# A fused linear-attention and feed-forward kernel: w_out words loaded 18 steps ahead, one q buffer per unit, and the left half of a group's output buffer in two pieces

## The chip, the core and the metric

The kernel runs on one core of a Trainium2 chip. The metric is device time in microseconds, the median of the runs of one kernel. The profile is one execution of the same program, recorded instruction by instruction; its times count from its own first instruction. TensorE is called PE, VectorE DVE, ScalarE ACT, GpSimd POOL and SyncE SP. SP does no arithmetic here: it issues nearly all transfers, one after the other. ACT issues the others, the stores of the middle result.

## The reference

The computation is linear attention with a norm for each head, followed by a feed-forward block without bias.

```python
kv = np.einsum('bhsd,bhse->bhde', k, v)           # batch 8, 8 heads, 576 tokens, head_dim 64
out = np.einsum('bhsd,bhde->bhse', q, kv)
rms = np.sqrt(np.mean(out * out, axis=-1, keepdims=True) + 1e-06)
x = (out / rms * g_norm)                          # reordered to 4608 tokens x 512
h = x @ w_in                                      # w_in 512 x 2048
sp = np.log1p(np.exp(h))                          # h itself above 20
out = (h * np.tanh(sp)) @ w_out                   # w_out 2048 x 512
```

The arrays are handed over as 64-bit floating point. The kernel reads the two weight matrices as pairs of 32-bit words and rebuilds a 32-bit value from each pair.

## The kernel before

**Two parts.** Part one goes through nine tiles of 512 tokens. For each tile it computes the attention, the first product and the activation, and stores the activated result in device memory (`gd`). Part two reads `gd` back in 18 pieces of 256 tokens and computes the second product. Part two starts about two thirds into the program, and no line of its loop is part of the change, but for the name of one buffer (`o_dst`, L607).

**Steps.** The first product of a tile is cut into four groups, and a group is computed with seven block products instead of eight (Strassen's scheme with sums and differences of blocks). One block product is one *step*: 12 matmuls at L411. So a group has 7 steps and a tile 28 (`NS`). The functions `p0` to `p6` (L371 to L398) are the steps of a group. They also move the accumulator out of PSUM: ACT copies blocks (L374, L379, L388), DVE adds blocks (L429), and ACT applies the activation, called Mish here (L116).

**The plan.** All other work is hung on a step number with `at(step, f)`, and `trace(step)` emits it when the step has been emitted: attention of the *next* tile (`attention(j)`, L498), conversion of `w_out` (L527), loads and stores. SP's order is exactly this order of emission. The orders on PE, ACT and DVE are made by a scheduler that estimates when each instruction can start; an engine then runs its list strictly in that order. A wait on one engine holds up all that stands behind it in the list.

**Attention.** A tile's attention is done in two units of four heads (two head pairs of two). A unit loads q (`load`, L267, eight pieces of one or two transfers), transposes it on DVE (L287), projects it with the product of k and v on PE (L299 to L304), squares (ACT, L308), sums over a head with a matrix of ones (PE, L319 to L322), takes the logarithm and the exponential on ACT (L327, L328) and multiplies on DVE (L332). From the third tile on, operands are split into a high and a low part first (`split`, L118: ACT L119, DVE L120). The logarithm and exponential need one table set on ACT and Mish another; each change is an `ACT_TABLE_LOAD`. Both units load q into one buffer, `qs`, so the second unit's load can't be issued before the first unit's transpose has read it.

**k and v.** They are loaded in four portions per tile (L206, L207), with one staging buffer for each. A portion is loaded when the product of the portion before it (L242) has been emitted.

**w_out.** Its conversion is cut into 16 halves (`weight_forms`, L126). Half `i` is loaded into a raw buffer (`w64`, two of them; L136), scaled on ACT (L141), joined on DVE (L146 to L148), turned into differences (L153 to L155), split into `wst` (one buffer; L119, L120) and stored in device memory (`wod`, L193). Half `i` is due 12 steps after half `i-1`. The line that sets the steps is

```python
for s, n in enumerate((-8, 0, 1, 2, 3, 4, 6)):   # load, scale, join, differences, first, rest, store
    at(max(NS, NS + 12 * i + n), run)
```

`w_in` is converted in the same way during the first tile, without a store, and before any attention needs the split buffers.

**The output buffers of a group.** `ul` (left 256 columns' two blocks: 11 and 21) and `ur` (12 and 22) hold 128 x 1024 values each, two of each. Block 11 is finished in step 5 of its group, block 22 in step 6, and block 21 in step 2 of the next group. `ur` is stored from step 7 on, counted from the group's start, and all of `ul` from step 10 on (L434, L427). The first write into the `ul` of a group two later is at step 14 (L374).

Of the kernel before, what the change touches and what calls it, by code (L numbers as in the profile page):

```python
# [29 lines left out]
def linear_attention_rms_mish_ffn(  # L30
# [95 lines left out]
    def weight_forms(srcs, m, n, forms, put=None):  # L126
# [10 lines left out]
            st["w"] = t.rearrange("p b n t -> p (b n) t")  # L137

        def scale():
            st["x"] = wpools["wx"].tile([P, 4 * w], F32, name="wx")  # L140
            nc.scalar.mul(st["x"], st["w"][:, :, 1].bitcast(F32), 2.0 ** -112)  # L141

        def join():
# [120 lines left out]
    def unit_steps(j, u):  # L264
        st = {}

        def load(n):  # L267
            if n == 0:
                st["q"] = att.tile([P, 2, T], F32, name="qs")
            a, i = divmod(n, 4)  # L270
            h, d0 = 4 * u + 2 * a + i // 2, 32 * (i % 2)
            for b, s0, cols in segments(j):
                n_ = cols.stop - cols.start
                nc.sync.dma_start(
                    st["q"][32 * i:32 * i + 32, a, cols].rearrange("p (c d) -> p c d", d=32),
                    q[b, h, s0:s0 + n_, d0:d0 + 32].rearrange("(c p) d -> p c d", p=32),
                )
# [137 lines left out]

    def u_dst(st, block):

        for name in ("ul", "ur"):
            if name not in st:
                st[name] = up.tile([P, 2, T], F32, name=name)  # L420
        return st["ul" if block[1] == "1" else "ur"][:, :, (int(block[0]) - 1) * TH:int(block[0]) * TH]

    def put_in(st, block, bank):
        o, i, n, t = u_dst(st, block), st["i"], st["n"], 7 * (NQ * st["i"] + st["n"])
        if block == "21":
            mish(o, bank)
            at(t + 10, lambda: nc.scalar.dma_start(gd[i][:, 2 * n:2 * n + 2, :], st["ul"]))  # L427
            return
        nc.vector.tensor_add(o, bank, o)  # L429
        if block == "11":  # L430
            mish(o, o)
        elif block == "22":
            mish(st["ur"], st["ur"])
            at(t + 7, lambda: nc.scalar.dma_start(gd[i][:, NF2 + 2 * n:NF2 + 2 * n + 2, :], st["ur"]))  # L434


    NS = 7 * NQ
# [12 lines left out]
    weight_pools(2, 1, 0)  # L450
    kv_new(0)
    rooms = [up.tile([P, 4, CM * D], F32, name=n) for n in ("ul", "ul", "ur", "ur")]
    units = {j: [unit_steps(j, u) for u in range(2)] for j in range(NT)}
    conv, kv_tiles = {}, {}
    for step in START.split():
# [8 lines left out]
        elif what == "k":  # L464
            ts = []
            for m in range(2):
                ts.append(rooms[2 * n + m])
                ts.append(x[0:SL, 2 * n + m, 0:4 * D].rearrange("p (h d) -> p h d", h=4))
# [29 lines left out]
    def attention(j):  # L498
# [14 lines left out]
        for u, ns in enumerate(((3, 5, 6, 8, 9, 10), (12, 14, 15, 17, 18, 19))):  # L513
            for s, n in enumerate(ns):
                at(t + n, units[j][u][s + 1])
            for n in range(8):
                at(t + 4 + n if u else max(t - 15 + 2 * n, n // 2 - 1), lambda u=u, n=n: units[j][u][0](n))
        at(t + 20, lambda: x_sums(0))
        for f, n in zip(range(7), (21, 22, 24, 25, 26, 27, 30)):
            at(t + n, lambda f=f: x_form(f))  # L520
# [4 lines left out]
        attention(j)  # L525
    at(NS - 1, lambda: weight_pools(2, 1, 1))
    for i in range(2 * NF2):  # L527
        for s, n in enumerate((-8, 0, 1, 2, 3, 4, 6)):
            def run(i=i, s=s):
                if s == 0:  # L530
                    conv["out", i] = weight_out(i // 2, i % 2)
                conv["out", i][s]()
            at(max(NS, NS + 12 * i + n), run)
# [70 lines left out]

    def o_dst(st, block):
        if "o" not in st:
            st["o"] = up.tile([P, 2, DM], F32, name="ul")  # L607
        r, c = int(block[0]) - 1, int(block[1]) - 1
        return st["o"][:, r, c * G:(c + 1) * G]

# [140 lines left out]
```

## Time and profile before

| | us |
|---|---|
| median of 3 runs (lowest, highest) | 957.74 (954.23, 961.63) |
| the profiled execution, its own time | 965.35 |
| the profiled execution, span of its instructions | 963.6 |
| PE busy / ACT busy / DVE busy in that span | 858.5 / 510.3 / 596.3 |
| part one up to the last steps of the first product | 0 to about 598 |
| part two in its steady course | 618.7 to the end |

How to read the rows of the views shown below. In a row of the list of instructions in time, the first number is the start, the second the length of the instructions merged in the row, then the engine (SPq and ACTq are the queues on which SP and ACT issue transfers), the line, the operation, what it writes and reads, and a count; in brackets stands how long the engine had been idle before, and what ended that. In the view of waits a row has the total of such idle times, their number and the longest. In the view of stretches a row has the stretch, its length, then the busy time of PE, of PE's weight loads, DVE, ACT and POOL, with the number of instructions, then the granted PE clock (1.00 is full speed), the busy share of the transfer engines, and GB/s.

### The profile page before, as it was taken

The numbers are of one execution on the slowest core, as the hardware profiler recorded it, in microseconds if no ns is written. First come the engines' busy times: TensorE is split into PE (matmuls) and PEld (weight loads), VectorE is DVE, ScalarE is ACT, GpSimd is POOL, SyncE is SP. The second block draws the span as 40 slices with busy tenths as digits, with TensorE's granted clock in tenths as the row PEclk, the third lists the DMA queues.
The fourth block names the chain that finished last, engine by engine and source line by source line (L and its number), as shares of the span: only waits on it lengthen the run. The fifth ranks groups of instructions, "written<-read, shape, count | busy, mean of one in ns | idle before, by whom it ended". The sixth has DMA issues, their size and how long they took to land.

```text
span 963.6 us, 16994 instructions
## 1 busy us (share of the span) xinstructions
PE 858.5 (89%) x6940; PEld 823.7 (85%) x6940; DVE 596.3 (62%) x832; ACT 510.3 (53%) x776; POOL 3.6 (0%) x14
## 2 busy tenths in 40 slices
PE   3587899698895987979989799799999999999998
PEld 1376798697895986978989699799999999999997
DVE  3777964637456556374764445766677766777762
ACT  2666775666556655665676535334444344444341
POOL 1000000000000000000000000000000000000000
PEclk9797999899996997989999899899999999999999
DMA  9567475666466665665653779634433345333421
GB/s 189 160 181 201 127 215 154 199 180 169 151 166 185 173 175 179 177 167 184 183 170 127 256 304 350 248 110 150 157 110 132 110 141 165 110 132 110 133 87 44
DMA packets 204461, 160.49 MB, mean 167 GB/s; under 512 B 91232, under 2 KB 189536, under 8 KB 203360
## 3 DMA queue, kind: packets, MB, share of 16 engines
q1 hardware_dynamic: 194016, 121.67, 43.4%
q10 hardware_dynamic: 10368, 37.75, 10.1%
q8 instruction: 54, 0.88, 0.4%
q14 instruction: 23, 0.19, 0.1%
HBM read 97.52 MB, written 61.87 MB: 165 GB/s over the span
## 4 chain that ended last, share of the span: by engine, by line
PE 44%; DMA 6%; ACT 2%; DVE 1%; issue 1%; SPq 0%; ACTq 0%
PE a L600 20%; PE bc L600 15%; PE a L411 4%; PE bc L411 3%; DMA g<-gd 2%; DMA gd<-ul 2%; DMA wf<-wod 1%; PE q L668 1%; DMA vm<-in_v_dram 1%; DMA wod<-wst 1%; DVE gf L120 0%; DMA w<-in_moe_w_out_dram 0%; ACT L116 0%; ACT fa L328 0%; ACT ur L116 0%
## 5 line engine op out<-in xcount | busy, mean ns | idle before, releaser
L411 PE MATMUL a<-gf,wf 128*128 128x256 f32 x1728 | 254.8, 302 | 49.2 <-ACT ul L116 18.0
L411 PEld LDWEIGHTS a<-gf,wf 128*128 128x128 f32 x1728 | 236.4, 207 | 60.1 <-ACT ul L116 20.2
L600 PE MATMUL a<-wf,gf 128*128 128x256 f32 x1632 | 204.7, 286 | 4.7 <-ACT ul L374 3.8
L600 PEld LDWEIGHTS a<-wf,gf 128*128 128x128 f32 x1632 | 200.8, 194 | 5.3 <-ACT ul L374 4.0
L411 PE MATMUL bc<-gf,wf 128*128 128x256 f32 x1296 | 183.3, 292 | 7.6 <-ACT ur L379 3.2
L411 PEld LDWEIGHTS bc<-gf,wf 128*128 128x128 f32 x1296 | 170.0, 198 | 11.4 <-ACT ur L379 4.7
L600 PE MATMUL bc<-wf,gf 128*128 128x256 f32 x1224 | 153.2, 284 | 1.2 <-DVE gf L120 1.2
L600 PEld LDWEIGHTS bc<-wf,gf 128*128 128x128 f32 x1224 | 149.9, 193 | 1.4 <-DVE gf L120 1.4
L120 DVE TENSOR_TENSOR gf<-g,gf 128x1024 fp32r<-128x1024 f32 (+1 forms) x100 | 109.6, 1103 | 64.9 <-ACT gf L119 64.7
L119 ACT CAST gf<-g 128x1024 fp32r<-128x1024 f32 (+1 forms) x100 | 94.4, 953 | 60.4 <-PE bc L600 55.2
L119 ACT CAST gf<-s 128x1024 fp32r<-128x1024 f32 (+2 forms) x58 | 49.1, 849 | 34.0 <-PE a L600 29.3
L120 DVE TENSOR_TENSOR gf<-s,gf 128x1024 fp32r<-128x1024 f32 (+2 forms) x58 | 56.3, 972 | 14.2 <-ACT gf L119 14.0
L374 ACT COPY ul<-a 128x512 f32<-128x512 f32 (+1 forms) x53 | 27.2, 516 | 60.2 <-PE a L600 29.3
L429 DVE TENSOR_TENSOR ur<-bc,ur 128x512 f32<-128x512 f32 x36 | 24.8, 688 | 37.6 <-PE bc L411 29.6
L116 ACT ACTIVATE ur<-ur 128x1024 f32<-128x1024 f32 x36 | 37.8, 1050 | 12.3 <-DVE ur L429 12.3
L146 DVE TENSOR_SCALAR wx<-wx 128x512 uint32<-128x512 uint32 (+1 forms) x24 | 12.3, 513 | 51.3 <-ACT wx L141 51.3
L120 DVE TENSOR_TENSOR fl<-fa,fh 128x1024 fp32r<-128x1024 f32 x28 | 34.2, 1220 | 13.5 <-ACT fh L119 13.4
L429 DVE TENSOR_TENSOR ur<-a,ur 128x512 f32<-128x512 f32 x36 | 24.7, 685 | 27.2 <-PE a L411 27.1
L141 ACT ACTIVATE wx<-w 128x512 f32<-128x512 f32 (+1 forms) x24 | 19.8, 826 | 38.3 <-DMA w<-in_moe_w_out_dram 29.9
L429 DVE TENSOR_TENSOR ul<-bc,ul 128x512 f32<-128x512 f32 x36 | 24.8, 688 | 24.7 <-ACT ul L374 16.1
L119 ACT CAST fh<-fa 128x1024 fp32r<-128x1024 f32 x28 | 29.3, 1047 | 16.8 <-DVE fa L287 16.6
L120 DVE TENSOR_TENSOR gf<-gf 128x512 fp32r<-128x512 f32 x45 | 29.9, 682 | 8.9 <-ACT gf L119 8.9
(95 smaller groups left out, 846.4 us busy)
## 6 DMA issues: line engine op xcount, KB each, us to landing
g<-gd SPq DMA_DIRECT2D x18, 2048.0 KB, 8.8
gd<-ur ACTq DMA_DIRECT2D x36, 512.0 KB, 4.1
gd<-ul ACTq DMA_DIRECT2D x36, 512.0 KB, 4.9
wod<-wst SPq DMA_DIRECT2D x16, 896.0 KB, 5.4
wf<-wod SPq DMA_DIRECT2D x8, 1792.0 KB, 12.0
out_dram<-ul SPq DMA_DIRECT2D x18, 512.0 KB, 2.8
w<-in_moe_w_in_dram SPq DMA_DIRECT2D x32, 256.0 KB, 3.9
w<-in_moe_w_out_dram SPq DMA_DIRECT2D x32, 256.0 KB, 3.5
```

Source lines behind the costliest of these rows:

```text
L116: in_turn(nc.scalar.activation(o, i, AF.Mish))
L119: nc.scalar.copy(hi, src)
L120: nc.vector.tensor_sub(lo, src, hi.bitcast(F32))
L141: nc.scalar.mul(st["x"], st["w"][:, :, 1].bitcast(F32), 2.0 ** -112)
L146: nc.vector.tensor_single_scalar(t, t, 3, ALU.logical_shift_left)
L374: nc.scalar.copy(dst(st, "11"), st["a"])
L411: nc.tensor.matmul(bank[:, jj], w[:, right, a, kc, :], xf[:, b, kc, :], start=first and jj == kc == s == 0, stop=(kc == 1 and s == 2), ski ...
L429: nc.vector.tensor_add(o, bank, o)
L600: nc.tensor.matmul(bank, gf[:, a, c, :], wo[c][:, right, b, :], start=first and c == s == 0, stop=(c == NF2 - 1 and s == 2), skip_group_ch ...
L668: nc.tensor.matmul(banks[b][:, h], gf[:, a, c, :], wo[2 * n + c][:, right, d, :], start=n == c == s == h == 0, stop=last_one, skip_group_c ...
```

## The change

Three things are changed, and some rooms move to make space.

1. **w_out words.** The load of half `i` moves from 8 to 18 steps before its conversion, and the store from 6 to 5 steps behind the conversion's start. The halves 0 and 1 are both loaded at the first step of the second tile.
2. **q buffers.** `qs` becomes `qs0` and `qs1`, one for each unit (a unit is a pair of head pairs). The first unit's pieces are loaded at 24 to 3 steps before the tile's steps, three steps apart (before: 15 to 1, two apart); the second unit's at 15 steps before to 6 steps into them, three apart (before: 4 to 11 steps into them, one apart).
3. **Left half.** `ul` is replaced by `ula` (block 11, first 256 tokens) and `ulb` (block 21, the other 256). Block 11 is stored on ACT's queue from step 6 on, block 21 from step 10 on, so a group has three stores and no longer two. A piece of the left half holds 256 KB and goes to rows of 1 KB in two places per partition; the whole left half was 512 KB.

The rooms: the scaled words of `w_in` use `fl`, a buffer of the attention, and `wx` is opened for `w_out` alone; the first tile's second portion of k and v is loaded into `x`, where the tile's result is later written; part two's output buffer is now called `ur`.

```diff
-            st["x"] = wpools["wx"].tile([P, 4 * w], F32, name="wx")
+            st["x"] = (wpools["wx"] if put else att).tile([P, 4 * w], F32, name="wx" if put else "fl")
...
-                st["q"] = att.tile([P, 2, T], F32, name="qs")
+                st["q"] = att.tile([P, 2, T], F32, name=f"qs{u}")
...
-        for name in ("ul", "ur"):
-            if name not in st:
-                st[name] = up.tile([P, 2, T], F32, name=name)
-        return st["ul" if block[1] == "1" else "ur"][:, :, (int(block[0]) - 1) * TH:int(block[0]) * TH]
+        name, shape = {"11": ("la", TH), "21": ("lb", TH)}.get(block, ("r", T))
+        if name not in st:
+            st[name] = up.tile([P, 2, shape], F32, name="u" + name)
+        return st[name] if name != "r" else st[name][:, :, (int(block[0]) - 1) * TH:int(block[0]) * TH]
...
         if block == "21":
             mish(o, bank)
-            at(t + 10, lambda: nc.scalar.dma_start(gd[i][:, 2 * n:2 * n + 2, :], st["ul"]))
+            at(t + 10, lambda: nc.scalar.dma_start(left[:, :, TH:T], o))
             return
         nc.vector.tensor_add(o, bank, o)
         if block == "11":
             mish(o, o)
+            at(t + 6, lambda: nc.scalar.dma_start(left[:, :, 0:TH], o))
...
-    rooms = [up.tile([P, 4, CM * D], F32, name=n) for n in ("ul", "ul", "ur", "ur")]
+    rooms = [up.tile([P, 4, CM * D], F32, name="ur") for _ in range(2)]
+    rooms += [x[:, 2 * u:2 * u + 2].rearrange("p a (h n) -> p (a h) n", h=2) for u in range(2)]
...
-                at(t + 4 + n if u else max(t - 15 + 2 * n, n // 2 - 1), lambda u=u, n=n: units[j][u][0](n))
+                at(max(t - (15 if u else 24) + 3 * n, n // 2 - 1), lambda u=u, n=n: units[j][u][0](n))
...
-        for s, n in enumerate((-8, 0, 1, 2, 3, 4, 6)):
+        for s, n in enumerate((-18, 0, 1, 2, 3, 4, 5)):
```

**What moves on SP.** The place is in the third tile, where the first portion of k and v of the fifth tile is issued. `km`, `kr`, `vm`, `vr` are the staging buffers of k and v, `qs` the q buffer, `w_...` a raw buffer of `w_out`, `wod_100` the stored forms. Before:

```order
L206 DMA km<-in_k_dram 128x2x256
L207 DMA kr<-in_k_dram 64x2x64
L206 DMA vm<-in_v_dram 128x2x256
L207 DMA vr<-in_v_dram 64x2x64
L274 DMA qs<-in_q_dram 32x6x32
L274 DMA qs<-in_q_dram 32x10x32
L136 DMA w_2060<-in_moe_w_out_dram 128x2x256 x2
L274 DMA qs<-in_q_dram 32x8x32 x2
L193 DMA wod_100<-wst 1792x1x128
L274 DMA qs<-in_q_dram 32x8x32 x10
L136 DMA w_2304<-in_moe_w_out_dram 128x2x256 x2
```

At the same place now:

```order
L206 DMA km<-in_k_dram 128x2x256
L207 DMA kr<-in_k_dram 64x2x64
L206 DMA vm<-in_v_dram 128x2x256
L207 DMA vr<-in_v_dram 64x2x64
L274 DMA qs_1864<-in_q_dram 32x8x32 x4
L274 DMA qs_2102<-in_q_dram 32x8x32 x2
L193 DMA wod_100<-wst 1792x1x128
L136 DMA w_2135<-in_moe_w_out_dram 128x2x256 x2
L274 DMA qs_1864<-in_q_dram 32x8x32 x2
L274 DMA qs_2102<-in_q_dram 32x8x32 x2
```

The store is that of half 3 in both. Before, the load of half 4 (`w_2060`) stood just ahead of it, and that of half 5 (`w_2304`) ten q transfers behind it. Now half 4 has been loaded further up, half 5 (`w_2135`) is loaded right behind the store, and the q transfers of the two units alternate.

**What moves on ACT.** The place is the end of the first tile and the start of the second. The numbers tell buffers apart: `ul_906`, `ul_1040` and `ul_1261` belong to three groups in a row, `a` is an accumulator, `gd0` and `gd1` the stored results of the first two tiles. Before:

```order
L119 CAST wst_1111<-w64_1062 128x4x128
L427 DMA gd0_90<-ul_906 128x1024
L250 CAST kvh0_1043<-s2_1125 64x64
L116 ACTIVATE ul_1040<-ul_1040 128x2x256
L116 ACTIVATE ur_1041<-ur_1041 128x1024
L374 COPY ul_1261<-a_1248 128x2x256
L434 DMA gd1_91<-ur_1041 128x1024
L308 ACTIVATE fa_1239<-x2_1195 128x1024
L141 ACTIVATE wx_1391<-w64_1177 128x512
```

Now, for the first of these three groups:

```order
L374 COPY ula_921<-a_908 128x512
L119 CAST wf_859<-w64_719 128x4x256
L119 CAST gf_108<-gf_107 128x512
L119 CAST gf_110<-gf_107 128x512
L116 ACTIVATE ula_921<-ula_921 128x512
L434 DMA gd0_90<-ula_921 128x2x256
L379 COPY ur_939<-bc_926 128x2x256
L119 CAST gf_108<-s1_904 128x512
```

Before, the copy into `ul_1261`, which takes the space of `ul_906`, stood four rows behind the store of `ul_906`. Now the store of `ula_921` follows its Mish at once, and the copy that takes its space, into `ula_1284`, stands 25 rows further down.

More of the change, by code (lines that the diff above doesn't have):

```diff
@@ L416, in u_dst @@
     def u_dst(st, block):
-        for name in ("ul", "ur"):
-            if name not in st:
-                st[name] = up.tile([P, 2, T], F32, name=name)
-        return st["ul" if block[1] == "1" else "ur"][:, :, (int(block[0]) - 1) * TH:int(block[0]) * TH]
+        name, shape = {"11": ("la", TH), "21": ("lb", TH)}.get(block, ("r", T))
+        if name not in st:
+            st[name] = up.tile([P, 2, shape], F32, name="u" + name)
+        return st[name] if name != "r" else st[name][:, :, (int(block[0]) - 1) * TH:int(block[0]) * TH]
     def put_in(st, block, bank):
         o, i, n, t = u_dst(st, block), st["i"], st["n"], 7 * (NQ * st["i"] + st["n"])
+        left, right = gd[i][:, 2 * n:2 * n + 2, :], gd[i][:, NF2 + 2 * n:NF2 + 2 * n + 2, :]
         if block == "21":
             mish(o, bank)
-            at(t + 10, lambda: nc.scalar.dma_start(gd[i][:, 2 * n:2 * n + 2, :], st["ul"]))
+            at(t + 10, lambda: nc.scalar.dma_start(left[:, :, TH:T], o))
             return
@@ L431, in put_in @@
             mish(o, o)
+            at(t + 6, lambda: nc.scalar.dma_start(left[:, :, 0:TH], o))
         elif block == "22":
-            mish(st["ur"], st["ur"])
-            at(t + 7, lambda: nc.scalar.dma_start(gd[i][:, NF2 + 2 * n:NF2 + 2 * n + 2, :], st["ur"]))
+            mish(st["r"], st["r"])
+            at(t + 7, lambda: nc.scalar.dma_start(right, st["r"]))
     NS = 7 * NQ
@@ L449, in linear_attention_rms_mish_ffn @@
     nc.gpsimd.memset(ones[D:P, D:P].bitcast(F32), 1.0)
-    weight_pools(2, 1, 0)
+    weight_pools(2, 0, 0)
     kv_new(0)
-    rooms = [up.tile([P, 4, CM * D], F32, name=n) for n in ("ul", "ul", "ur", "ur")]
+    rooms = [up.tile([P, 4, CM * D], F32, name="ur") for _ in range(2)]
+    rooms += [x[:, 2 * u:2 * u + 2].rearrange("p a (h n) -> p (a h) n", h=2) for u in range(2)]
+    rrooms = [up.tile([SL, 4, D], F32, name=n) for n in ("ula", "ula", "ulb", "ulb")]
     units = {j: [unit_steps(j, u) for u in range(2)] for j in range(NT)}
@@ L467, in linear_attention_rms_mish_ffn @@
                 ts.append(rooms[2 * n + m])
-                ts.append(x[0:SL, 2 * n + m, 0:4 * D].rearrange("p (h d) -> p h d", h=4))
+                ts.append(rrooms[2 * n + m])
             kv_tiles[n] = kv_load(0, 4 * n, 4, ts)
@@ L606, in o_dst @@
         if "o" not in st:
-            st["o"] = up.tile([P, 2, DM], F32, name="ul")
+            st["o"] = up.tile([P, 2, DM], F32, name="ur")
         r, c = int(block[0]) - 1, int(block[1]) - 1
```

## The prediction

> **What bounds the kernel now.** I read the stretches of the program first, cut at the tiles of part one.
>
> ```profile
> core 0: us, PE busy (x) PEld busy (x) DVE busy (x) ACT busy (x) POOL busy (x), PEclk, DMA share, GB/s
> 0.00:118.60 118.60, 79.06 (x555) 64.52 (x556) 83.84 (x121) 70.19 (x109) 3.58 (x14) 0.86 0.67 174
> 118.60:170.60 52.00, 49.39 (x440) 47.19 (x438) 30.45 (x57) 31.91 (x52) 0.00 (x0) 1.00 0.61 172
> 170.60:227.70 57.10, 49.28 (x417) 47.73 (x413) 31.37 (x55) 37.34 (x60) 0.00 (x0) 0.94 0.62 182
> 227.70:287.00 59.30, 52.81 (x438) 49.52 (x439) 31.94 (x56) 36.45 (x59) 0.00 (x0) 0.94 0.58 172
> 287.00:351.00 64.00, 53.42 (x449) 51.02 (x448) 34.92 (x59) 38.83 (x61) 0.00 (x0) 0.87 0.61 174
> 351.00:415.80 64.80, 56.01 (x448) 53.03 (x447) 35.36 (x62) 39.08 (x64) 0.00 (x0) 0.89 0.62 178
> 415.80:475.90 60.10, 53.29 (x442) 49.60 (x441) 35.43 (x64) 39.82 (x65) 0.00 (x0) 0.94 0.66 191
> 475.90:527.80 51.90, 47.46 (x360) 45.95 (x359) 32.56 (x50) 38.32 (x55) 0.00 (x0) 0.97 0.47 143
> 527.80:584.10 56.30, 49.78 (x381) 48.58 (x380) 24.58 (x49) 26.54 (x47) 0.00 (x0) 0.94 0.74 280
> 618.70:963.60 344.90, 340.08 (x2808) 339.68 (x2808) 234.48 (x229) 135.76 (x179) 0.00 (x0) 0.99 0.36 118
> ```
>
> PE is the busiest engine everywhere. In the last row (part two) it is busy for 340.08 of 344.90 us at a clock of 0.99: nothing is to be had there, and the change doesn't touch it. In the eight rows ahead of it, tiles that do nearly the same work take 51.9 to 64.8 us. Two reach 52; the others lose 5.1, 7.3, 12.0, 12.8, 8.1 and 4.3 us against 52, in sum 49.6 us. The slow tiles have more idle PE and a lower clock. ACT is busy for some 60% of them, so it isn't short of time, but it works its list in order. So I read its waits next.
>
> ```profile
> ACT wx L141 <- DMA w<-in_moe_w_out_dram: 29.9, 11, 4.7
> ACT ul L374 <- DMA gd<-ul: 27.3, 14, 4.3
> ACT wst L119 <- DMA wod<-wst: 11.1, 7, 3.4
> DVE fa L287 <- DMA qs<-in_q_dram: 6.7, 5, 2.0
> SPq L274 <- DVE fa L287: 16.1, 6, 9.0
> ```
>
> ACT stands for 29.9 us before words of w_out that have not landed, and for 27.3 us before a left half that has not been stored. DVE waits for q, and SP, with w_out words queued behind it, waits until a transpose frees the one q buffer. Last I looked for PE's stalls and for what ACT did ahead of each.
>
> ```profile
> 173.78 0.66 ACT L141 ACTIVATE wx<-w 128x512 f32<-128x512 f32 x1 [4.07 <-DMA w<-in_moe_w_out_dram]
> 178.81 5.49 PE L411 MATMUL a<-gf,wf 128*128 128x256 f32 x24 [6.47 <-ACT ul L116]
> 230.69 0.66 ACT L141 ACTIVATE wx<-w 128x512 f32<-128x512 f32 x1 [3.08 <-DMA w<-in_moe_w_out_dram]
> 232.46 2.93 PE L411 MATMUL a<-gf,wf 128*128 128x256 f32 x12 [2.18 <-DVE ur L429]
> 247.45 0.58 ACT L374 COPY ul<-a 128x512 f32<-128x512 f32 x1 [2.52 <-DMA gd<-ul]
> 248.09 0.38 PE L411 MATMUL a<-gf,wf 128*128 128x256 f32 x1 [2.72 <-ACT ul L374]
> 294.30 0.66 ACT L141 ACTIVATE wx<-w 128x512 f32<-128x512 f32 x1 [3.36 <-DMA w<-in_moe_w_out_dram]
> 297.33 0.80 PE L321 MATMUL s<-fl,ones 128*128 128x512 f32 x1 [6.01 <-DVE fl L120]
> 352.18 0.67 ACT L141 ACTIVATE wx<-w 128x512 f32<-128x512 f32 x1 [3.72 <-DMA w<-in_moe_w_out_dram]
> 356.88 0.50 PE L321 MATMUL s<-fl,ones 128*128 128x512 f32 x1 [2.83 <-DVE fl L120]
> 423.41 0.66 ACT L141 ACTIVATE wx<-w 128x512 f32<-128x512 f32 x1 [4.68 <-DMA w<-in_moe_w_out_dram]
> 425.19 2.93 PE L411 MATMUL a<-gf,wf 128*128 128x256 f32 x12 [3.59 <-DVE ur L429]
> 546.43 0.58 ACT L374 COPY ul<-a 128x512 f32<-128x512 f32 x1 [4.32 <-DMA gd<-ul]
> 547.07 2.93 PE L411 MATMUL a<-gf,wf 128*128 128x256 f32 x12 [2.92 <-ACT ul L374]
> 561.30 1.60 PE L411 MATMUL a<-gf,wf 128*128 128x256 f32 x12
> ```
>
> Each PE stall stands 1 to 5 us behind an ACT wait for a transfer. And a stall costs twice: the 12 matmuls behind it take 2.93 us where an undisturbed dozen takes 1.60.
>
> **The change part by part.** *Words of w_out 18 steps ahead.* The wait of ACT goes if the words have landed by the time of L141. At 52 us for 28 steps a step is 1.9 us, so the ten steps gained are 19 us; the longest wait was 4.7. And the load no longer stands behind ten q transfers. I take all these waits as gone. What each was worth: of the stall of 6.47 at 178.81 the 4.07 that ACT waited (the rest, 2.40, is the chain of exponential, table load and Mish), and the slow dozens behind it, 5.49 against 1.60 + 1.60, so 2.3; at 232.46 all 2.18, with 2.93 - 1.60 = 1.33 of slow clock; at 297.33 the 3.36 that ACT waited; at 356.88 all 2.83; at 425.19 all 3.59 and 1.33. In sum 4.07 + 2.3 + 3.51 + 3.36 + 2.83 + 4.92 = 21.0 us. What is late next is that chain behind the logarithm, which the change doesn't touch.
>
> The Trainium skill, "TensorE: Matmul & The Clock Gate", section "HAM oscillation", says that PE should have no idle gap above some 3.4 us, since its clock falls back then. By that rule the stalls of 2.18 and 2.92 us would not have slowed what follows, and the sum would be 2.7 us smaller; the rows show 2.93 us behind both, so the rows decide.
>
> *The left half in two.*
>
> ```profile
> gd<-ul ACTq DMA_DIRECT2D x36, 512.0 KB, 4.9
> w<-in_moe_w_out_dram SPq DMA_DIRECT2D x32, 256.0 KB, 3.5
> 178.79 0.33 ACTq L427 DMA_DIRECT2D gd<-ul  x1
> ```
>
> Where Mish runs on time, the first piece is on its way four steps earlier and nothing waits for it. But after a table load ACT runs the Mishes of two groups in a burst, and there the store starts only 1 to 2 us earlier; being of 256 KB it should also land about 1.4 us sooner (4.9 against 3.5, an estimate, since one is a store and the other a load). So I count the 2.52 at 248.09 in full, and of the stall at 547.07, where ACT waited 4.32 us, half of 2.92 and the slow clock, 1.33: in sum 5.3 us. Between nothing and the 27.3 us of the wait, the PE rows are the nearest. The 36 more stores take ACT's queue 36 x 0.33 = 11.9 us if nothing hides them; the issue at 178.79 lies inside a Mish, so I charge 1. The Mish or cast behind the store in ACT's list is what would wait.
>
> The Trainium skill, "DMA: Bandwidth & Descriptors", section "Bandwidth", speaks against the split: it wants transfers of 1 MiB and more, and its fixed cost of about 2 us per transfer is paid once more by each group. By its formula a piece of 256 KB lands only 0.6 us sooner than 512 KB, an estimate, and I would count about 1 us less.
>
> *Two q buffers.* DVE's waits for q (6.7 us) and SP's for the transpose (16.1 us) go. No PE stall above has a q wait straight ahead of it, so the value lies between 0 and 6.7; I take 3, for the head start of the attention chain.
>
> *Forms of w_out.* `wst` stays one buffer; its store moves from step 6 to 5. The 11.1 us of waits may shrink or grow; I count 0.
>
> *The start.* In the first tile the second unit's q now goes out ahead of the second portion of k and v (8 transfers more) and of the next words of w_in (12 more).
>
> ```profile
> 43.25 4.62 SPq L274 DMA_DIRECT2D qs<-in_q_dram  x8
> 53.60 1.96 SPq L136 DMA_DIRECT2D w<-in_moe_w_in_dram  x4
> w<-in_moe_w_in_dram SPq DMA_DIRECT2D x32, 256.0 KB, 3.9
> 68.15 1.15 ACT L141 ACTIVATE wx<-w 128x1024 f32<-128x1024 f32 x1
> 62.51 0.44 PE L299 MATMUL x<-fh,kvh 128*128 128x64 f32 x2 [2.05 <-DVE fh L287]
> ```
>
> One q transfer takes SP 4.62 / 8 = 0.58 us. The words of w_in landed at 53.60 + 1.96 + 3.9 = 59.5 and were used at 68.15: 8.7 us of cover for 12 x 0.58 = 7.0. k and v come 4.6 us later, and so does the first unit's q, for which PE waits 2.05 us already; its products now stand later in PE's list. I charge 2, between 0 and the 7.0. The rooms in `x` make the first normalization wait for a product that ends within a microsecond of it; with the other renamings I put that at nothing, since the cover is the table load that follows, and at 1 without it.
>
> **Sum.** -21.0 - 5.3 - 3 + 1 + 2 = -26.3 us. Against the profiled execution (965.35 us; span 963.6) that gives 939. It lies 7.6 above the median of the runs, 957.74, to which the same gain is applied: 931.4, so 931. The check from above: 26 is about half of the 49.6 us that the slow tiles lose. If part one ends earlier, the reload for part two moves with it, because each load waits for the weights of a group to be used up.
>
> **The rivals.** *All tiles at the best pace.* ACT, freed of its waits, also empties the small stalls that I left out, and every tile takes 52 us: -49.6, so 908. For it speaks that the tiles at 118.60 and 475.90 do so already; against it, that the chain of exponential, table load and Mish remains.
>
> *The wait moves to the forms.* With the words always there, ACT scales them sooner and then stands before the one `wst` buffer until the last forms are stored; the words' 29.9 us turn up at L119. Then only the left half and q are gained: -5.3 - 3 + 3 = -5.3, so 952. For it speaks the wait of 11.1 us at that place; against it, that SP reaches the store without q waits now.
>
> *Slower: transposes let loose.* q always being there, the scheduler puts DVE's 16 transposes of the later tiles earlier, before their target buffer is free, and DVE's additions, which free PSUM for PE, queue behind the wait. Each must cost (26.3 + 9.6) / 16 = 2.2 us before the kernel is slower by 1%. At 2.5 us, the loss is 40: -26 + 40 = +14, so 971. DVE's longest wait for q was 2.0, so such a length is possible; against it, DVE has slack (31 to 35 us busy in most tiles of 52 to 65).
>
> *No effect.* The words are late anyway, as SP waits for k and v staging and not for q: 958.
>
> **How the numbers follow.** Forecast 0.58, at 931 with its own range of 915 to 947 (21.0 could be two thirds or one and a half times as much). Best pace 0.12, moved wait 0.15, slower 0.11, no effect 0.04. The range from 907 to 960 leaves out the slower case and a few hundredths of the best pace, under 2 in 10. A measurement here can tell about 1% from no change: faster means below 948.2, slower above 967.3. Faster: 0.56 of the forecast, 0.12 and 0.05 of the moved wait, 0.73. Slower: 0.09 of the slower case. Same: the rest, 0.18.
>
> **What would show it.** In the profile after, the row of ACT's L141 waiting for w_out should be gone or below 3 us, that of L374 for the left half below 12, L119 for `wod` not above 11, and the tiles from 170 us on should take 52 to 57 us at a clock of 0.95 or more. The first 118.6 us should be within 3 us of that. Part two should stay at 345. The forecast is wrong if the waits go and the tiles stay as long (another engine was behind PE's stalls), or if a new row of more than 20 us stands among ACT's or DVE's waits in part one.

## The result, and the profile after

The changed kernel takes 931.92 us in the median of four runs (930.05 to 938.03), the kernel before 959.68 us beside it (954.23 to 966.08). The ratio is 0.9719 with a 95% interval of 0.9642 to 0.9797: faster. A second set of six runs, made later for comparison, gave 928.12 us and 0.9672 (0.9623 to 0.9721). Ratios are taken from the fast runs alone, so they differ a little from the quotients of the medians. The forecast was 931, with a range of 907 to 960. The number came out; as the runs below show, the terms of which it was the sum did not.

The stretches of the changed kernel, cut like those of before:

```profile
core 0: us, PE busy (x) PEld busy (x) DVE busy (x) ACT busy (x) POOL busy (x), PEclk, DMA share, GB/s
0.00:128.90 128.90, 86.00 (x555) 69.27 (x556) 84.45 (x122) 71.02 (x109) 3.59 (x14) 0.84 0.65 170
128.90:180.60 51.70, 49.47 (x441) 47.03 (x439) 31.67 (x59) 34.27 (x54) 0.00 (x0) 1.00 0.60 165
180.60:234.90 54.30, 49.30 (x436) 46.89 (x436) 35.36 (x61) 40.36 (x65) 0.00 (x0) 0.99 0.71 198
234.90:286.60 51.70, 50.41 (x424) 48.98 (x425) 30.98 (x55) 33.66 (x56) 0.00 (x0) 0.95 0.70 199
286.60:354.00 67.40, 54.25 (x475) 51.73 (x473) 40.28 (x70) 45.51 (x71) 0.00 (x0) 0.92 0.68 187
354.00:408.50 54.50, 52.35 (x449) 50.72 (x449) 33.13 (x58) 39.04 (x62) 0.00 (x0) 0.95 0.68 189
408.50:462.10 53.60, 48.84 (x409) 46.87 (x410) 33.52 (x61) 35.92 (x60) 0.00 (x0) 0.97 0.80 224
462.10:513.10 51.00, 46.34 (x361) 45.42 (x360) 27.52 (x38) 34.56 (x48) 0.00 (x0) 0.97 0.32 109
513.10:560.50 47.40, 44.56 (x350) 42.64 (x350) 24.76 (x49) 27.23 (x49) 0.00 (x0) 1.00 0.88 331
594.00:936.20 342.20, 337.47 (x2808) 337.06 (x2808) 235.78 (x233) 138.15 (x181) 0.00 (x0) 1.00 0.36 121
```

The start has become 10.3 us longer (128.9 against 118.6), most tiles have come down to 51 to 55 us, one is still 67.4 (its cut holds 475 matmuls, the others 350 to 449), and part two keeps its pace (342.2 us against 344.9 for the same 2808 matmuls). Since such cuts do not hold equal work, another mark is used from here on: ACT's first copy of an accumulator into a tile's left half (L374). From the second tile's copy to the last tile's, seven tiles on, lies what is called *the middle* below. This mark is not exact either, because PE is not always equally far when ACT comes to it. Between the two marks the traces hold some 2400 to 2450 matmuls of L411, and at 1.60 us for twelve that alone can make some 6 us.

The waits of the changed kernel that answer to those of before:

```profile
ACT wst L119 <- DMA wod<-wst: 35.7, 14, 6.2
ACT wx L141 <- DMA w<-in_moe_w_out_dram: 9.4, 6, 2.3
ACT ula L374 <- DMA gd<-ula: 1.6, 1, 1.6
DVE fa L287 <- DMA qs<-in_q_dram: 0.4, 1, 0.4
SPq L274 <- DVE fa L287: 4.2, 1, 4.2
```

ACT's wait for the words has fallen from 29.9 to 9.4 us, but its wait for the one `wst` buffer, until the forms of the half before are stored, has grown from 11.1 to 35.7. The two together were 41.0 and are 45.1. The left half's wait (27.3) is all but gone, and so are DVE's wait for q from the third tile on (6.7) and most of SP's wait for a transpose (16.1). Behind the grown wait PE stalls, as it did behind the words:

```profile
415.64 0.62 ACT L119 CAST wst<-w 128x512 fp32r<-128x512 f32 x1 [5.42 <-DMA wod<-wst]
416.67 1.04 ACT L119 CAST fh<-fa 128x1024 fp32r<-128x1024 f32 x1
417.76 0.74 PE L302 MATMUL x<-fh,kvl 128*128 128x448 f32 x1 [4.51 <-ACT fh L119]
```

So the words' 21 us of the forecast can hardly be what was gained. Three explanations were to be told apart: the forecast's terms; the words' wait only moves, and left half and q carry the gain; or the new order of the engines' lists brings it by chance.

### The profile page after: what moved, and what is told of

It reads as the page before. It is cut to its first block, busy times and chain, and to the rows that moved or that the text cites. A ratio compares the mean times of both kernels' runs of the same rounds, so it can differ in the third digit from the quotient of the medians.

```text
span 936.2 us, 17021 instructions
## 1 busy us (share of the span) xinstructions
PE 849.1 (91%) x6940; PEld 816.1 (87%) x6940; DVE 597.0 (64%) x832; ACT 512.8 (55%) x776; POOL 3.6 (0%) x14
## 4 chain that ended last, share of the span: by engine, by line
PE 70%; DMA 12%; SPq 6%; ACT 6%; DVE 3%; issue 2%; ACTq 0%; DVEq 0%
PE a L605 21%; PE bc L605 16%; PE a L411 16%; PE bc L411 11%; DMA w<-in_moe_w_out_dram 5%; SPq L274 3%; DMA w<-in_moe_w_in_dram 2%; SPq L136 2%; PE s L242 2%; PE q L673 2%; DMA qs<-in_q_dram 1%; DMA wod<-wst 1%; ACT L116 1%; ACT gf L119 1%; PE x L302 1%
## 5 line engine op out<-in xcount | busy, mean ns | idle before, releaser
L411 PE MATMUL a<-gf,wf 128*128 128x256 f32 x1728 | 248.1, 297 | 38.7 <-ACT ulb L116 22.3
L411 PEld LDWEIGHTS a<-gf,wf 128*128 128x128 f32 x1728 | 231.2, 202 | 47.1 <-ACT ulb L116 24.0
L605 PE MATMUL a<-wf,gf 128*128 128x256 f32 x1632 | 202.5, 283 | 2.3 <-ACT ur L374 1.3
L605 PEld LDWEIGHTS a<-wf,gf 128*128 128x128 f32 x1632 | 198.6, 192 | 2.9 <-ACT ur L374 1.5
L411 PE MATMUL bc<-gf,wf 128*128 128x256 f32 x1296 | 185.3, 292 | 8.4 <-ACT ur L379 3.8
L411 PEld LDWEIGHTS bc<-gf,wf 128*128 128x128 f32 x1296 | 171.7, 198 | 12.6 <-ACT ur L379 4.2
L120 DVE TENSOR_TENSOR gf<-g,gf 128x1024 fp32r<-128x1024 f32 (+1 forms) x100 | 109.5, 1104 | 63.2 <-ACT gf L119 62.8
L119 ACT CAST gf<-g 128x1024 fp32r<-128x1024 f32 (+1 forms) x100 | 94.7, 955 | 58.9 <-PE bc L605 52.4
L119 ACT CAST gf<-s 128x1024 fp32r<-128x1024 f32 (+2 forms) x58 | 49.4, 851 | 39.3 <-PE a L605 28.0
L120 DVE TENSOR_TENSOR gf<-s,gf 128x1024 fp32r<-128x1024 f32 (+2 forms) x58 | 56.4, 973 | 17.4 <-ACT gf L119 17.2
L388 ACT COPY ur<-a 128x512 f32<-128x512 f32 (+1 forms) x53 | 27.4, 517 | 35.2 <-PE a L605 26.0
L379 ACT COPY ur<-bc 128x512 f32<-128x512 f32 (+1 forms) x53 | 27.4, 517 | 35.2 <-PE bc L605 24.3
L120 DVE TENSOR_TENSOR fl<-fa,fh 128x1024 fp32r<-128x1024 f32 x28 | 34.2, 1222 | 14.6 <-ACT fh L119 14.3
L120 DVE TENSOR_TENSOR gf<-gf 128x512 fp32r<-128x512 f32 x45 | 30.6, 689 | 6.3 <-ACT gf L119 6.2
L431 DVE TENSOR_TENSOR ula<-bc,ula 128x512 f32<-128x512 f32 x36 | 24.7, 687 | 12.5 <-PE bc L411 9.9
L308 ACT ACTIVATE fa<-x 128x1024 f32<-128x1024 f32 x18 | 18.4, 1025 | 25.2 <-PE x L304 18.8
L120 DVE TENSOR_TENSOR wst<-w,wst 128x512 fp32r<-128x512 f32 x16 | 11.0, 691 | 32.3 <-ACT wst L119 32.2
```

Of the source, the lines that this page charges most:

```text
L119: nc.scalar.copy(hi, src)
L120: nc.vector.tensor_sub(lo, src, hi.bitcast(F32))
L379: nc.scalar.copy(dst(st, "22"), st["c"])
L388: nc.scalar.copy(dst(st, "12"), st["a"])
L411: nc.tensor.matmul(bank[:, jj], w[:, right, a, kc, :], xf[:, b, kc, :], start=first and jj == kc == s == 0, stop=(kc == 1 and s == 2), ski ...
L605: nc.tensor.matmul(bank, gf[:, a, c, :], wo[c][:, right, b, :], start=first and c == s == 0, stop=(c == NF2 - 1 and s == 2), skip_group_ch ...
```

## The experiments

All ratios are to the kernel before, run beside each on the same chip. The single parts and the forms' wait were run on one chip, the pairs, the q buffers and the start on a second, the last store, the kernel without conversion and the second set of the changed kernel on a third.

| kernel | words | left | q | ratio (95%) | start | middle | rest |
|---|---|---|---|---|---|---|---|
| before | | | | 1 | 115.6 | 430.8 | 417.1 |
| words only | x | | | 1.0084 (1.0050 to 1.0118) | 116.7 | 431.5 | 419.8 |
| left half only | | x | | 0.9910 (0.9879 to 0.9941) | 117.2 | 410.6 | 420.0 |
| q only | | | x | 0.9831 (0.9779 to 0.9884) | 124.2 | 401.6 | 416.6 |
| q buffers, old steps | | | part | 0.9924 (0.9896 to 0.9952) | 115.9 | 422.2 | 413.1 |
| words and q | x | | x | 0.9828 (0.9785 to 0.9871) | 126.2 | 402.5 | 415.8 |
| left half and q | | x | x | 0.9752 (0.9709 to 0.9795) | 125.0 | 392.0 | 418.3 |
| changed kernel, first profile | x | x | x | 0.9719 (0.9642 to 0.9797) | 128.0 | 397.3 | 410.9 |
| changed kernel, second profile | x | x | x | 0.9672 (0.9623 to 0.9721) | 122.8 | 395.9 | 410.9 |

The last three columns are us of one profiled execution: up to the second tile's first copy, the middle, and from the last tile's first copy to the end of the span. Such an execution lies up to 8 us from its kernel's median (965.35 of before lies above its own, 938.03 of the changed kernel too), so the ratios say how much, and the columns roughly where.

**Words alone.** Only the line of the steps is changed:

```diff
-        for s, n in enumerate((-8, 0, 1, 2, 3, 4, 6)):
+        for s, n in enumerate((-18, 0, 1, 2, 3, 4, 5)):
```

> The kernel before with the one line of the w_out steps changed (words 18 steps ahead, store at step 5) and nothing else. Theory 1 (the prediction's sum): ACT's waits for the words, 29.9 us, go, and 21 us of PE stalls with them: about 937 us median against 958 to 960 of the kernel before. Theory 2 (the wait moves): the row of ACT waiting at L119 for wod, 11.1 us before and 35.7 us in the changed kernel, takes over 25 us here too, ACT's two waits together stay near 41, and the time stays within 5 us of before; the gain of the whole change then comes from the left half and q. Both expect the first 118.6 us to stay.

It is slower, 969.38 us against 962.42; the loss is under 1%, but the whole interval of the ratio lies above 1. Its waits:

```profile
ACT wst L119 <- DMA wod<-wst: 33.4, 13, 4.8
ACT fh L119 <- DVE fa L287: 13.6, 6, 5.5
ACT ul L374 <- DMA gd<-ul: 12.1, 5, 5.1
ACT wx L141 <- DMA w<-in_moe_w_out_dram: 3.7, 3, 1.4
```

The wait for words is gone (29.9 to 3.7), and the one for forms has taken its place (11.1 to 33.4): 37.1 together, 41.0 before. The middle is as long as before. Theory 2 had the move of the wait right; neither foresaw a loss. A second reading is in the row of L374: the left half's wait fell from 27.3 to 12.1 here although nothing was done for it, and the time did not fall with it. A total of waits on ACT is no price.

**Left half alone.** `u_dst`, `put_in` and the rooms of the first tile as in the changed kernel, the steps of words and q as before.

> The kernel before with the left half in two buffers and two stores and the rooms of the first tile that go with it; words and q as before. Theory 1 (the prediction's sum): 5.3 us less, the 36 stores cost about 1: 953 to 956 us, and the words' wait of about 30 us stays. Theory 2 (the left half carries the change): L374's wait of 27.3 us goes and nearly all of it was PE's: 15 to 25 us less, 935 to 945. The rooms in x: theory 1 charges the start nothing; if the 10 us that the changed kernel starts later (second tile's products at 128.9 us, before 118.6) come from them, the second tile starts near 129 here.

The ratio 0.9910 is 8.7 us on 962; its profile, at 949.69 the fastest of its runs, has the middle 20.2 us shorter. By the ratio the gain lies between the theories, nearer the first: more than 5.3, less than 15. Its waits:

```profile
ACT wx L141 <- DMA w<-in_moe_w_out_dram: 34.8, 13, 5.5
ACT ula L374 <- DMA gd<-ula: 10.5, 3, 4.7
```

More than a third of the left half's wait is still there, and so is all of the wait for words, as theory 1 had it. The place of the second tile, 117.2, clears the rooms of the late start.

**q alone.** Two buffers, the new steps, and the scaled words of `w_in` in `fl`.

> The kernel before with a q buffer for each unit, the new q steps, and the scaled words of w_in in fl; words of w_out and left half as before. Theory 1 (the prediction's sum): 3 us less for the waits for q and 2 more at the start: 957 to 959 us, no change. Theory 2: SP's wait of 16.1 us behind the transpose holds up words and stores, so that without it ACT's waits for words (29.9) and forms (11.1) shrink together below 25 and the time falls by 8 or more. If the late start of the changed kernel comes from the order of q at the start, the second tile's products begin near 129 us here instead of 118.6, and the sum is 8 us worse by that.

This is the largest part: 0.9831, or 16 us, in spite of a start that is 8.6 us later. One row that it removed stood in the profile before, and the prediction did not quote it:

```profile
ACT fh L119 <- DVE fa L287: 16.6, 5, 5.5
```

In the kernel before, ACT, which splits the transposed q (`fh` from `fa`), stood 16.6 us waiting for DVE's transposes, since q came late. With q alone changed:

```profile
ACT wx L141 <- DMA w<-in_moe_w_out_dram: 27.0, 14, 4.0
ACT ul L374 <- DMA gd<-ul: 11.5, 6, 5.1
ACT wst L119 <- DMA wod<-wst: 3.6, 4, 1.9
ACT fh L119 <- DVE fa L287: 0.6, 1, 0.6
```

The wait for the transposes is gone, the wait for words still stands at 27.0, and yet the middle is 29.2 us shorter. Theory 2 expected words and forms together below 25; they are 30.6, so its reason does not hold, though its number does.

It would be easy to take those 16.6 us for the price of the late q. But PE did not stand behind them. The longest of these waits before, and all engines during it:

```profile
156.48 1.05 ACT L119 CAST fh<-fa 128x1024 fp32r<-128x1024 f32 x1 [5.52 <-DVE fa L287]
150.96:156.48 5.52, 5.52 (x48) 5.52 (x47) 2.57 (x4) 0.00 (x1) 0.00 (x0) 1.00 0.34 115
```

PE is busy for all 5.52 us, and for the 5 us that follow; it is so too in the waits of 4.73 and 4.32 us. The row of 16.6 is a sign that q is late, and no price. What moves with the time is the place of the second unit's transpose (L287): on the average of the seven tiles it starts 32.5 us behind the copy that marks a tile's start in the kernel before, and 25.5 us behind it here. So the second half of the next tile's attention is done sooner. That PE's stalls go for this reason is argued from these rows and not shown by a run.

**The buffer or the steps.** As q alone, but with q loaded at its old steps, so that SP's order is that of before:

```diff
-                st["q"] = att.tile([P, 2, T], F32, name="qs")
+                st["q"] = att.tile([P, 2, T], F32, name=f"qs{u}")
...
                 at(t + 4 + n if u else max(t - 15 + 2 * n, n // 2 - 1), lambda u=u, n=n: units[j][u][0](n))
```

> The kernel before with a q buffer for each unit (and w_in words scaled in fl to make room), but q loaded at the old steps: SP's order of issues is that of the kernel before. With the new q steps as well the ratio is 0.9831, the first write of a group's left half in the second tile stands at 124.2 us (before 115.6), and from there to the same place of the last tile it takes 401.6 us (before 430.8). Theory 1 (the wait for the one buffer was the cost: SP 16.1 us behind the transpose, ACT 16.6 us behind it): the wait goes with the buffer alone, the start stays near 116, the ratio is 0.975 to 0.98. Theory 2 (the steps count: q came too late after the buffer was free, eight transfers in a row): most of the gain is gone, 0.993 or more, and the start stays near 116.

0.9924: a little under half. SP no longer waits for a transpose, but ACT still does, and the second unit's transpose starts 30.8 us behind the mark:

```profile
ACT wx L141 <- DMA w<-in_moe_w_out_dram: 30.1, 12, 5.4
ACT fh L119 <- DVE fa L287: 14.3, 4, 5.5
```

The steps bring the rest, although they also make the start late (115.9 here): it is with the earlier loads that ACT's wait goes and the transpose comes sooner. Theory 1 is out; theory 2 put its bound at 0.993, and the interval holds it.

**Pairs.** The changed kernel without the left half, and without the words:

> The changed kernel without the split of the left half (one buffer of 512 KB, stored as a whole, k and v of the first tile in the old rooms). If the parts add up, 1.0084 + 0.9831 - 1 = 0.9915. Theory A (words worth nothing beside q, left half worth 0.9%): 0.981 to 0.985. Theory B (what is saved beyond the sum comes from words and left half together): 0.990 or more.

> The changed kernel with the w_out steps put back (words 8 steps ahead, store at step 6), so left half and q alone. The single parts gave ratios to before of 1.0084 (words), 0.9910 (left half) and 0.9831 (q); their sum is 0.9825 and the whole change has 0.972, so the parts help one another somewhere. Theory A (the words are worth nothing, their wait only moves to the forms): left half and q together give all of it, 0.970 to 0.974, and ACT's wait for words is back near 30 us without harm. Theory B (the words pay once left half and q are there): 0.977 or more, so 5 us or more slower than the changed kernel.

The words can now be read in three pairs of rows of the table. In the middle they bring +0.7 us (alone), +0.9 (beside q) and +3.9 to +5.3 (beside left half and q). So no gain in part one shows in any company, and for words and q together (0.9828) theory A holds. Yet the kernel with left half and q alone came out at 938.04, 6 us above the changed one's first median: its ratio, 0.9752, lies between the theories, and its interval overlaps that of the changed kernel. In the profiles the difference is in the last column, 418.3 against 410.9. ACT at the end of part one, left half and q:

```profile
560.83 0.41 ACT L119 CAST gf<-s 128x256 fp32r<-128x256 f32 x1
569.58 0.37 ACTq L429 DMA_DIRECT2D gd<-ulb  x1
569.99 0.40 ACT L119 CAST gf<-g 128x256 fp32r<-128x256 f32 x1 [8.75 <-DMA gd<-ur]
574.51 3.57 PE L605 MATMUL a<-wf,gf 128*128 128x256 f32 x15 [6.47 <-DVE gf L120]
```

The very last store of a left half is held back until an earlier store of `ur` has landed. The casts behind it, which part two needs, wait 8.75 us, and PE waits 6.47 behind them. The changed kernel issues the same store without a wait.

**The last store.** Left half and q, and that one store on SP's queue:

```diff
-            at(t + 10, lambda: nc.scalar.dma_start(left[:, :, TH:T], o))
+            at(t + 10, lambda: (nc.scalar if 4 * i + n < 35 else nc.sync).dma_start(left[:, :, TH:T], o))
```

> The kernel with left half and q changed and the words not (ratio 0.9752, 938 us), with one transfer moved: the store of the very last block 21 goes out on SP's queue, behind the last reload of weights, and no longer on ACT's. The lists of PE and DVE stay word for word the same, ACT's loses one row. In that kernel's profile ACT stands for 8.75 us at 569.99, until an earlier store of ur has landed, because this last store had to be issued first; PE stands behind it, while stores take some 18 us to land beside the reload. Theory 1: that stall is on the path, so it alone sets the end: 929 to 931 us, ratio 0.966 to 0.968. Theory 2: the reload of 8 x 1792 KB sets the end anyway: within 2 us of 938.

928.36 us, ratio 0.9660 (0.9623 to 0.9697), against 0.9752: theory 1, by a little more than it forecast. ACT and PE at the same place:

```profile
561.08 0.41 ACT L119 CAST gf<-g 128x256 fp32r<-128x256 f32 x1 [0.86 <-DVE g L579]
567.46 2.05 PE L605 MATMUL a<-wf,gf 128*128 128x256 f32 x15 [0.44 <-DVE gf L120]
```

This is the cleanest pair here, because in the two traces PE, DVE and ACT run the same instructions in the same order: one stall of 8.75 us on ACT is worth 0.9%. The two kernels ran on different chips, each beside the kernel before, but 7.5 us of the 8.8 between their profiles lie in the last column (418.3 against 410.8). And the pair bears on the words: without them and without that stall the kernel is as fast as the changed one (0.9660; the changed one 0.9672 beside it). What the words gave the whole change was, as far as these runs show, that its last store did not happen to wait.

**The forms' wait.** The changed kernel with the forms stored from ACT's queue (`nc.sync` to `nc.scalar` in `store` of `weight_out`).

> The changed kernel with the forms of w_out stored from ACT's queue instead of SP's; nothing else. In the changed kernel the store of one half was issued at 285.03 us behind 12 transfers of q on SP (278.90 to 284.93), and ACT stood for 6.24 us until it had landed; such waits sum to 35.7. Theory 1 (SP's queue makes the store late, and the wait is on the path): the wait falls below 12 us and the time by the PE stalls that stand behind these waits, 4.51 at 417.76, 2.85 at 293.56 and 1.53 at 347.02, in all about 9 us: 923. Theory 2 (the wait is cover for others, or the store only moves in ACT's own list): the time stays within 4 us of the changed kernel's 932.

```profile
ACT wx L141 <- DMA w<-in_moe_w_out_dram: 18.1, 7, 4.7
ACT gf L119 <- DMA gd<-ur: 8.3, 1, 8.3
ACT wst L119 <- DMA wod<-wst: 0.9, 1, 0.9
```

The forms' wait goes from 35.7 to 0.9, and part of it is back as a wait for words (9.4 to 18.1). The middle is 395.5 us, hardly shorter than the 395.9 and 397.3 of the changed kernel: more than halving ACT's waits for the conversion, from 45.1 to 19.0, gave nothing that shows. Theory 2. The time, 934.49 and 0.9729 (0.9677 to 0.9782), also holds the stall at the last store (8.3), which this kernel has and the changed one hasn't.

**The conversion's whole cost.** The kernel before, without the conversion of 15 of the 16 halves; part two multiplies with the forms of the first half throughout:

```diff
+                if i == 0 or s == 0:
+                    conv["out", i][s]()
+                elif s == 6:
+                    nc.sync.dma_start(
+                        wod[i // 2][:, :, :, i % 2 * P:(i % 2 + 1) * P],
+                        kept[0].rearrange("p f s m n -> p f s (m n)").bitcast(F32))
-                conv["out", i][s]()
```

> The kernel before without the conversion of 15 of the 16 halves of w_out: their words are loaded as before, but not scaled, joined, subtracted or split, and the forms of half 0 are stored 16 times. So part two computes with wrong weights at the same pace; what is left out is 15 times the work on ACT (some 2.5 us each, 37 us) and DVE, and all 41.0 us of ACT's waits for words and forms. Theory 1 (the prediction: the words' waits stall PE for 21 us): at least 21 us less, ratio 0.978 or lower. Theory 2 (ACT has slack, the waits are mostly cover): ratio 0.985 or higher, though waits and work are both gone.

923.76 us against 961.3, ratio 0.9622 (0.9586 to 0.9658): 37.5 us for all of it, and a middle of 391.8 us, as short as that of left half and q with the whole conversion. Theory 2 is out: waits and work of the conversion together do cost PE. They are 41.0 us of waits and about 30 of work (15/16 of 10.7 + 9.9 + 6.5 + 4.8, the four shapes of L141 and L119 in ACT's groups), so about half of the 71 us that ACT was freed of reached the end. DVE was freed too, of some 63 us of work (15/16 of the rows of L146 to L155 and of `wst` at L120, 67 us). How the 37.5 divide between ACT's waits, ACT's work and DVE's work this kernel can't say, and so it can't price the words' waits alone; the kernels above say that shifting the wait from one line to another, or halving it, is not enough. The next wait on DVE is in the profile already, q in its one buffer (30.6 us, 6.7 before). ACT's wait for the transposes is nearly what it was, and the middle is short all the same:

```profile
DVE fa L289 <- DMA qs<-in_q_dram: 30.6, 8, 6.3
ACT fh L119 <- DVE fa L289: 14.3, 7, 3.4
```

**The start.** The changed kernel with the second unit's q of the second tile at its old steps, and then the same beside left half, q and the last store:

```diff
-                at(max(t - (15 if u else 24) + 3 * n, n // 2 - 1), lambda u=u, n=n: units[j][u][0](n))
+                at(t + 4 + n if u and j == 1 else max(t - (15 if u else 24) + 3 * n, n // 2 - 1), lambda u=u, n=n: units[j][u][0](n))
```

> The changed kernel with the second unit's q of the second tile loaded at its old steps (4 to 11), all else as changed. In the changed kernel the second tile's first left-half write stands at 128.0 us, before at 115.6, and with left half alone at 117.2. Theory 1 (20 transfers ahead of k, v and the words of w_in make the start late): 117 to 119 us there, and the program ends 8 to 11 us sooner, ratio 0.961 to 0.964. Theory 2 (another thing delays the start, the rooms together with q, or the scaled words in fl): the place stays above 124, ratio 0.970 to 0.974. Theory 3 (the start comes back, but the reload for part two, during which the transfer engines are busy to 0.96 and more from 540 to 590 us, keeps the end where it is): place near 118, ratio 0.970 or more.

> As the kernel with left half and q alone and the last store on SP's queue, and in addition the second unit's q of the second tile at its old steps, 4 to 11. With all three parts that start came back by 9.2 us (128.0 to 118.8 at the second tile's first left-half write), but the time stayed (932.3 against 931.9 of the changed kernel). Theory 1 (both gains hold where the reload doesn't take them): place at 118 to 120, 921 to 925 us, ratio 0.957 to 0.962, so the best of all kernels here. Theory 2 (what the start gives, the tiles lose: their conversion and k, v loads come no sooner): 929 to 933, ratio 0.966 to 0.971.

The second tile's first copy in the changed kernel and with the old steps for that one unit:

```profile
128.04 0.59 ACT L374 COPY ula<-a 128x512 f32<-128x512 f32 x1
```

```profile
118.81 0.59 ACT L374 COPY ula<-a 128x512 f32<-128x512 f32 x1 [1.14 <-PE a L411]
```

In all, the seven profiles with the new order at the start have that copy at 122.0 to 128.0 us (mean 124.7), the seven that keep the old order there, the kernel without conversion (118.3), this one and the next among them, at 115.6 to 118.8 (mean 117.2). So the order of q makes the start 7.5 us late by this mark, and theory 1 has the cause right. Some of it is the mark's: in five of the seven, 319 matmuls of L411 stand ahead of the copy and not 302, which is some 2 us. But the time did not follow: 932.26 us, 0.9707 (0.9663 to 0.9752), no better than the changed kernel. Place and ratio are those of theory 3, but not its reason: the last column is 411.1, as in the changed kernel, so nothing is lost at the reload. The middle of that profile is 400.1, some 3 to 4 us longer, and the changed kernel's second profile has its copy at 122.8 by itself. Beside left half, q and the last store the same edit brings the place to 117.6 and the time from 928.36 to 925.19 (0.9642, 0.9599 to 0.9685). That lies between the two theories. It is the lowest time of a kernel that does the whole work, but the interval holds the ratio of the kernel without the edit, and that of the changed kernel (928.12 beside it); none of them beats the changed one by more than can be measured.

> The changed kernel itself, for comparison on the same chip: 0.964 to 0.980 to before, 932 us, by its first four runs. Its profiled execution then was the longest of the four (938); a usual one should show where it differs.

## Why the prediction was right, and where it was wrong

**Words, -21.0: wrong.** The step that failed is "I take all these waits as gone. What each was worth". Most of the waits for the words did go (9.4 of 29.9 us are left). But each price was read off a PE stall a few us behind the wait, and the next wait on ACT stood at the same place: the one `wst` buffer, with the store of the forms late in SP's queue. What is late next was said to be the chain behind the logarithm; it was the forms. Measured, the words are worth +8 us alone, nothing beside q, and beside left half and q, as far as the runs show, only the chance of the last store. The mechanism is that of the rival "the wait moves to the forms"; its row (L119 above 11) came as described, and so did the forecast's own sign of failure, a new row of more than 20 us. Its time, 952, did not come, because the terms left to it were too small.

**Left half, -5.3: right in kind, too small.** 8.7 us alone (0.9910), 0.8% beside q. The step that was too small is "the PE rows are the nearest": two stalls were counted. Where the rest came from was not traced. Stalls of PE below 1 us are not it, for in the middle they sum to 8.2 us before and to 7.7 with the left half changed. The charge of 1 for 36 more stores can't be seen apart.

**q, -3, and the start, +2: wrong by the size.** q with its start is worth 16 us alone and 15 beside the left half. The failed step is "No PE stall above has a q wait straight ahead of it". It asks for a stall right behind a wait, and the bounds, 0 to 6.7, came from DVE's row alone. The runs show that this row is no bound (16 us came), and that ACT's wait for the transposes (16.6 us, with PE busy meanwhile) is not the price either. They show the gain where q is loaded earlier and the second unit's transpose starts 5 to 7 us sooner in a tile; by what path this reaches PE stays open. In the middle PE's stalls above 1 us fall from 16 (42.7 us) to 8 (20.2 us) with q alone. The start was charged 2 between 0 and 7.0 and measured 7.5, or some 6 without the mark's share, near the upper end of its bounds; which of the loads that went out later holds it up was not tested.

**The forms at 0.** The wait grew by 24.6 us. That it costs 0 as long as nothing else changes fits the middle of the kernel that stores from ACT, but is not shown by it alone, since part of the wait is back there as a wait for words.

**The reload "moves with it": not always.** Left half and q had the last tile's first copy at 517.0, 8.4 us ahead of the changed kernel's first profile, and lost nearly all of it (418.3 against 410.9) at the last store beside the reload.

**The clock** counts, as forecast: the middle loses busy time of PE as well as idle time.

```profile
115.60:546.40 430.80, 377.68 (x3099) 358.91 (x3097) 243.94 (x414) 275.20 (x433) 0.00 (x0) 0.94 0.59 173
```

```profile
122.80:518.70 395.90, 362.14 (x3063) 346.94 (x3063) 241.06 (x408) 272.19 (x426) 0.00 (x0) 0.97 0.65 184
```

Before and in the changed kernel's second profile, 34.9 us lie between the two: 19.4 of idle PE (53.1 against 33.8) and 15.5 of busy PE, as the granted clock goes from 0.94 to 0.97. Some 4 us of the 15.5 are the mark's, with 36 matmuls fewer. The price of 1.33 us of slow clock behind each stall was too simple: behind some stalls as long it is nothing (last section).

**Other rivals.** Transposes let loose did not come: in the changed kernel DVE's transposes wait for q 0.4 us from the third tile on and 5.0 us ahead of it (2.5 before), and no new wait for a target buffer stands ahead of them. Best pace came for some tiles, not all; the tile of 67.4 us has two of the longest waits for forms in it (6.24 and 4.75 us). Open is why the words alone cost 0.8%. In the traces each edit but that of the last store changes the order of the lists of PE, DVE and ACT, and what that does by itself was not measured apart; for parts worth under 1%, the left half among them, it remains a rival.

So the sum was right by luck, through errors that cancel: the 21 us of the words did not come, while left half and q with the start and the stores brought 23.4 (961.39 to 938.04) instead of 5.3, and the changed kernel was spared most of the 8 to 9 us that the stall at the last store cost the kernel without the words. The range held for the same reason.

## What to carry to other kernels

A wait that stands ahead of a stall is not its price: before a term is credited, ask which buffer or transfer the same engine reaches next, and whether that one is ready. A late input is not priced by its own wait either, nor by the wait of the next engine: loading q earlier was worth 16 us where DVE waited 6.7 for it, and PE was busy through ACT's 16.6. To price such a part, change it alone. And where an engine that feeds the next phase also issues stores, look at the last ones: beside a saturating reload one held-back store of 256 KB cost as much as a whole part of the change gained.

## What the runs showed of the hardware

**Stores beside a reload take two to four times as long to land.** In the changed kernel, over the whole program and in the window from 535 to 575 us alone:

```profile
gd<-ur ACTq DMA_DIRECT2D x36, 512.0 KB, 4.4
gd<-ula ACTq DMA_DIRECT2D x36, 256.0 KB, 3.5
gd<-ulb ACTq DMA_DIRECT2D x36, 256.0 KB, 3.9
```

```profile
q1 hardware_dynamic: 966, 12.22, 74.0%
gd<-ur ACTq DMA_DIRECT2D x4, 512.0 KB, 8.5
gd<-ulb ACTq DMA_DIRECT2D x4, 256.0 KB, 13.6
gd<-ula ACTq DMA_DIRECT2D x3, 256.0 KB, 12.5
```

ACT issues these stores and SP the reload (the queue `q1`), and the stores are late all the same. The transfer engines are busy for 0.94 of that window. The Trainium skill, "DMA: Bandwidth & Descriptors", section "Issuing engines are not separate DMA queues", says that all of them run on the same 16 engines whoever starts them; the rows fit that. Why the last store of `ulb` had to wait for the landing of a store of `ur` in some kernels and not in others the profile doesn't show, and it stays open.

**Stalls of 2 to 3 us can halve the clock, or leave it whole.** Two stalls of the changed kernel, and in the last row one of the kernel with the last store on SP's queue:

```profile
83.94 2.93 PE L411 MATMUL a<-gf,wf 128*128 128x256 f32 x12 [3.02 <-DVE ur L431]
408.47 3.13 PE L411 MATMUL a<-gf,wf 128*128 128x256 f32 x24 [2.15 <-ACT ulb L116]
81.72 1.70 PE L411 MATMUL a<-gf,wf 128*128 128x256 f32 x12 [2.98 <-DVE ur L431]
```

A dozen takes 2.93 us behind a stall of 3.02, but 3.13 / 2 = 1.57 behind one of 2.15 and 1.70 behind one of 2.98. In the prediction's rows a stall of 2.18 was followed by 2.93. So the length of a stall does not decide alone at these lengths, and what does was not measured.

**One program, two starts.** The second tile's first copy came 5.2 us apart in the changed kernel's two profiles (128.0 and 122.8), with the same instructions in the same order on PE, ACT and DVE; half of one per cent can come from there alone.
